# Four edits to a gated recurrence followed by a two-layer network: touched words ahead of the loads, half turns of f, forget ahead of drive, and a last store in two

## The chip, the cores and the metric

The kernel runs on one core of one Trainium2 chip. The metric is the device time of that core in microseconds (us), and lower is better. Before the change the median of nine runs is 398.76 us (397.35 to 399.07).

A core has a matrix engine (TensorE, PE in the profile; PEld is its weight load), a vector engine (VectorE, DVE), an activation engine (ScalarE, ACT), a general engine (GpSimd, POOL), and a sequencer that mostly issues transfers (SyncE, SP). Each runs its own instructions in order and waits on semaphores for the others. Transfers (DMAs) are issued by SP, ACT or POOL and carried out by 16 DMA engines. Matrix results land in PSUM, all other tiles are in SBUF, and inputs and outputs are in HBM.

## What is computed

```python
sig = 1.0 / (1.0 + np.exp(-f_logit))
f = lower_bound[None, None, :] + (1.0 - lower_bound[None, None, :]) * sig
i = 1.0 - f
for t in range(S):
    h = f[:, t] * h + i[:, t] * x[:, t]
    y[:, t] = h
...
h1 = y @ w1
h2 = y @ w2
out = np.maximum(h1, h2) @ w_out
```

x and f_logit are 4 x 6144 x 256 in float32, lower_bound has 256 values, w1 and w2 are 256 x 1024 and w_out is 1024 x 256. The output has 24576 rows of 256. The recurrence runs along the 6144 tokens of each of the four sequences. With y as its result, the second part is a network of two layers whose hidden layer takes the larger of two products.

## The kernel before

The kernel writes the maximum as `h1 + relu(h2 - h1)`. So `wd`, the scaled difference of w2 and w1, feeds a relu, and the linear part `w1 @ w_out` is one 256 x 256 matrix, `w13`. The factor `1 - lower_bound` is taken out of the scan and put into these weights (`om`; `nom` is its negative). Per channel there is then a gate `u = sigmoid(-f_logit)`, a drive `v = u * x`, a forget factor `ff = 1 + nom * u`, and a scan `y = ff * y + v`.

The 24576 tokens are 48 blocks of 512 (`TB`). A block has its channels on the partitions in two halves of 128 (`KC`). Its work on TensorE is eight hidden units, each of two 512-column matmuls (line 254, into a PSUM tile `dT`, of which there are five), and a projection of forty 256-column matmuls (line 277, into `psO`). ACT does the relu of each unit (line 249) and the gate (206). DVE does the drive (210), forget (141), scan (152) and the copies of outputs out of PSUM (326).

**Start.** The loads are issued by SP in the order of the string `LOADS` (line 454). f0a and x0a are the first halves of block 0; w12 is quarter 2 of w1; w22 and w20 are quarters of w2; wo2 is a quarter of w_out. Only `lbr`, the row of lower bounds, is issued by ACT ahead of its first activation (line 570). A handwritten string, `PLAN` (line 458), orders all instructions of blocks 0 to 2 and of the weights, on all engines. In it, `G` is a gate, `V` a drive, `TU` and `TV` turns of u and v on TensorE, `F` a forget, `S` a scan, `RW`, `RO`, `D`, `SC`, `TW` and `KW` prepare weights, `H` is a hidden unit, `R` a relu, and `warm` stands for matmuls on a zero tile that keep TensorE busy. The first instruction of TensorE after the opening warm-up is `keeps_T`, which needs lbr.

**Completion semaphores.** The program uses eight of them in turn for the DMAs of SP and ACT together, in the order in which the program issues them. A DMA that takes a semaphore is issued only when the DMA that had it last has landed.

**Blocks from 3 on.** They reach SBUF by another way, in chunks: three chunks of one block (blocks 3, 4, 5), then chunks of two. `cast` (170) has POOL issue two DMAs that read f and x of a chunk and write them as bf16 to one of two spare places in HBM. `turn_dma` (180) has SP issue two transposing DMAs that bring f and then x of the chunk into SBUF with the channels on the partitions (`fT`, `xT`). `cast_behind` (189) has POOL copy one element of the turned f to `held`, which makes POOL wait for the turn, and then issue the next cast. The first cast waits in the same manner for the second half of x of block 1 (`CA` in the plan).

**Steady loop.** For each block from 3 on and each of its eight units, the loop from line 584 issues the hidden unit, an eighth of the projection of the block before, and at fixed units the copies, the sends (`send_out`, on SP), and for a later block the gate, drive, forget and scan. `gate_of` and `turn_of` say at which unit. SP's order is thus f turn, x turn, then some four sends per chunk. The last block's second half is stored a row set at a time (`store_row`, 339); the sends before it, the last block's first half among them, are `send_out`.

Of the kernel before, what the change touches and what calls it, by code (L numbers as in the profile page):

```python
# [8 lines left out]
FP32 = mybir.dt.float32  # L9
# [3 lines left out]
P = 128  # L13
# [3 lines left out]
def kernel(  # L17
# [13 lines left out]
    nc = tc.nc  # L31
# [4 lines left out]
    KC = D // P  # L36
    FC = DFF // P
    TB = 512
    HB = TB // 2
    NQ = TB // P  # L40
    NBB = S // TB
    NBLK = B * NBB
# [3 lines left out]
    CHUNKS = [(NP + i, 1) for i in range(CB * 2 - 1)]  # L46
# [3 lines left out]
    NS = 2  # L50

    const = ctx.enter_context(tc.tile_pool(name="const", bufs=1))
# [21 lines left out]
    om = const.tile([P, KC], FP32)  # L74
    nom = const.tile([P, KC], FP32)
    lbr = const.tile([KC, P], FP32)
    w1n = wpool.tile([P, KC, DFF], FP32)
    w1b = wpool.tile([P, KC, DFF], BF16)
    w2n = wpool.tile([P, KC, DFF], FP32)
# [10 lines left out]
    def alloc_in(j):  # L90
        fn = inpool.tile([P, NQ, D], FP32, name="fn")
        xn = inpool.tile([P, NQ, D], FP32, name="xn")
        ins[j] = (fn, xn)
        us[j] = natpool.tile([P, NQ, D], BF16, name="un")
        vs[j] = natpool.tile([P, NQ, D], BF16, name="vn")
        ffs[j] = nffpool.tile([P, KC, TB], BF16, name="nff")
        ys[j] = ypool.tile([P, KC, TB], BF16, name="y")

    def load(j, s, half=None):

        src = (f_logit, x)[s]
        q0, q1 = (0, NQ) if half is None else (2 * half, 2 * half + 2)
        nc.sync.dma_start(  # L103
            out=ins[j][s][:, q0:q1, :],
            in_=src[0, j * TB + q0 * P : j * TB + q1 * P, :].rearrange(
                "(q p) d -> p q d", p=P
            ),
        )
# [26 lines left out]
    def forget(o, i, h, on_act=False):  # L135
        if on_act:
            nc.scalar.activation(
                out=o, in_=i, func=AF.Identity, bias=1.0, scale=nom[:, h : h + 1]
            )
            return  # L140
        nc.vector.tensor_scalar(  # L141
            out=o, in0=i, scalar1=nom[:, h : h + 1], scalar2=1.0, op0=ALU.mult, op1=ALU.add
        )

    def scan(j, h, t0, t1, v):
# [18 lines left out]
    spare = {  # L164
        (k, name): scratch.tile([CB * TB, D], BF16, name=f"{name}{k}")
        for k in range(NS)
        for name in ("fs", "xs")
    }

    def cast(c):  # L170
        b0, n = CHUNKS[c]
        b, k = divmod(b0, NBB)
        for name, src in (("fs", f_logit), ("xs", x)):
            nc.gpsimd.dma_start(  # L174
                out=spare[c % NS, name][0 : n * TB, :],
                in_=src[b, k * TB : (k + n) * TB, :],
                max_dma_last_dim=4096,
            )

    def turn_dma(c):  # L180
        n = CHUNKS[c][1]
        for s, name in enumerate(("fs", "xs")):
            t = ttpool.tile([P, KC, CB * TB], BF16, name=("fT", "xT")[s])
            turned[c, s] = t
            nc.sync.dma_start_transpose(  # L185
                out=t[:, :, 0 : n * TB], in_=spare[c % NS, name][0 : n * TB, :]
            )

    def cast_behind(c):

        if c + 1 < NCH:
            last = CHUNKS[c][1] * TB - 1
            nc.gpsimd.tensor_copy(out=held[:], in_=turned[c, 0][:, KC - 1, last : last + 1])  # L193
            cast(c + 1)

# [2 lines left out]
    def part(j, s):  # L198
        c, o = home[j]
        return turned[c, s][:, :, o * TB : (o + 1) * TB]  # L200

    def gate(j):
        ffs[j] = midpool.tile([P, KC, TB], BF16, name="ff")
        ys[j] = ypool.tile([P, KC, TB], BF16, name="y")
        us[j] = midpool.tile([P, KC, TB], BF16, name="u")
        nc.scalar.activation(out=us[j][:], in_=part(j, 0), func=AF.Sigmoid, scale=-1.0)  # L206

    def drive(j):
        vs[j] = midpool.tile([P, KC, TB], BF16, name="v")
        nc.vector.tensor_tensor(out=vs[j][:], in0=us[j][:], in1=part(j, 1), op=ALU.mult)  # L210

    def forget_half(j, h, on_act=False):
        forget(ffs[j][:, h, :], us[j][:, h, :], h, on_act)

    def scan_half(j, h):
        scan(j, h, 0, TB, vs[j][:, h, :])
# [45 lines left out]
    def hidden(j, fc):  # L262
        hidden_whole(j, fc)
        relu(j, fc)
# [49 lines left out]
    def project(j, slot):  # L314
        i, half_ = divmod(slot, 2)
        n = FC + KC
        project_steps(j, i, half_ * n // 2, (half_ + 1) * n // 2)

    osbs = {}

    def copy_out(j, g, on_act=False):
# [3 lines left out]
        else:  # L325
            nc.vector.tensor_copy(out=osbs[j, g][:], in_=pos[j, g, 0][:])  # L326

    def send_out(j, g):
        r0 = j * TB + 2 * g * P
        nc.sync.dma_start(  # L330
            out=out[r0 : r0 + 2 * P, :].rearrange("(p r) d -> p r d", r=2),
            in_=osbs[j, g][:],
        )

    def store(j, g):
        copy_out(j, g)
        outs.append((j, g))

    def store_row(j, g, r):
        osb = lastpool.tile([P, D], FP32, name="row")  # L340
        nc.vector.tensor_copy(out=osb[:], in_=pos[j, g, r][:, 0, :])  # L341
        r0 = j * TB + 2 * g * P
        nc.sync.dma_start(
            out=out[r0 : r0 + 2 * P, :].rearrange("(p r) d -> p r d", r=2)[:, r, :],
            in_=osb[:],
        )
# [4 lines left out]
    def weight_load(k, w, src):  # L351
        cols = slice(k * QF, (k + 1) * QF)
        nc.sync.dma_start(
            out=w[:, :, cols], in_=src[:, cols].rearrange("(h p) f -> p h f", p=P)
        )

    def wout_load(k):
        nc.sync.dma_start(
            out=won[:, 2 * k : 2 * k + 2, :],
            in_=moe_w_out[k * QF : (k + 1) * QF, :].rearrange("(q p) c -> p q c", p=P),  # L360
        )
# [78 lines left out]
    def keep_warm(n):  # L440
        for _ in range(n):
            nc.tensor.matmul(  # L442
                idle[:].rearrange("p r d -> p (r d)"),
                lhsT=warm[:, 0:P],
                rhs=warm[:],
                start=True,
                stop=True,
            )
# [5 lines left out]
    LOADS = """  # L454
# [22 lines left out]
    def load_item(name):  # L477
        if name[:2] == "wo":
            wout_load(int(name[2]))
        elif name[0] == "w":  # L480
            w, src = ((w1n, moe_w1), (w2n, moe_w2))[int(name[1]) - 1]
            weight_load(int(name[2]), w, src)
        else:
            half = ("ab".index(name[2]),) if len(name) == 3 else ()
            load(int(name[1]), "fx".index(name[0]), *half)
# [3 lines left out]
    def send_pending(n):  # L489

        for _ in range(min(n, len(outs))):
            send_out(*outs.pop(0))
# [74 lines left out]
    with tc.manual_schedule():  # L567
        for j in range(NP):
            alloc_in(j)
        nc.scalar.dma_start(out=lbr[:], in_=lower_bound.rearrange("(h p) -> h p", p=P))  # L570
        for name in LOADS.split():
            load_item(name)
        nc.vector.memset(warm[:], 0.0)  # L573
        make_identity(nc, ident[:])
        nc.vector.tensor_copy(out=ident_b[:], in_=ident[:])
        keep_warm(7)
        for item in PLAN.split():
            issue(item)
        for c in range(1, 4):
            cast_behind(c)  # L580
            if c < 3:
                turn_dma(c + 1)

        for j in range(3, NBLK + 1):
            for fc in range(FC):
                if j < NBLK:
                    hidden(j, fc)
                project(j - 1, fc)
                if fc == 0 and j > 3:
                    store(j - 2, 1)  # L590
                if fc == 4 and j < NBLK:
                    store(j - 1, 0)
                if j > 4 and fc in (0, 4):
                    send_pending(2)
                if j == NBLK and fc in (3, 5, 7):
                    if fc == 3:
                        store(j - 1, 0)
                        send_pending(2)
                    else:
                        store_row(j - 1, 1, (fc - 5) // 2)  # L600
                if (j, fc) in gate_of:
                    b = gate_of[j, fc]
                    gate(b)
                    drive(b)
                    for h in range(KC):
                        forget_half(b, h)
                        scan_half(b, h)
                if (j, fc) in turn_of:
                    turn_dma(turn_of[j, fc])
                    cast_behind(turn_of[j, fc])  # L610
# [30 lines left out]
```

## Time and profile before

| | |
|---|---|
| median of nine runs | 398.76 us |
| lowest and highest | 397.35 and 399.07 us |
| time of the profiled execution | 398.48 us |
| span of it, first to last instruction | 396.7 us |
| TensorE clock granted | 1.0 of full |
| bytes moved by DMA | 79.12 MB |
| share of 16 DMA engines: queue of SP / of POOL | 58.2% / 36.4% |
| busy share of DMA engines, 0 to 25, 25 to 57, 57 to 103 us | 0.93, 0.86, 1.12 |

The busy time of an engine is the time in which an instruction of it runs. A wait is the idle time ahead of an instruction, put down to what came last. The chain of waits follows the program back from its last instruction, and at each step goes to what released it. Profile lines in the timeline and the chain begin with the start in us and the length in us; in the timeline a run of like instructions is merged (x4), and the brackets at the end hold the idle time ahead of the first and its releaser. The list of waits gives the sum in us, the number of waits and the longest. The share of DMA can pass 1, since packets of several queues overlap on an engine.

### The profile page before, as it was taken

The numbers are of one execution on the slowest core, as the hardware profiler recorded it, in microseconds if no ns is written. First come the engines' busy times: TensorE is split into PE (matmuls) and PEld (weight loads), VectorE is DVE, ScalarE is ACT, GpSimd is POOL, SyncE is SP. The second block draws the span as 40 slices with busy tenths as digits, with TensorE's granted clock in tenths as the row PEclk, the third lists the DMA queues.
The fourth block names the chain that finished last, engine by engine and source line by source line (L and its number), as shares of the span: only waits on it lengthen the run. The fifth ranks groups of instructions, "written<-read, shape, count | busy, mean of one in ns | idle before, by whom it ended". The sixth has DMA issues, their size and how long they took to land.

```text
span 396.7 us, 7107 instructions
## 1 busy us (share of the span) xinstructions
PE 387.3 (98%) x2779; PEld 273.5 (69%) x2825; DVE 251.3 (63%) x363; ACT 272.8 (69%) x450; POOL 38.4 (10%) x87
## 2 busy tenths in 40 slices
PE   7999999999999999999999999999999999999996
PEld 3786766676677766677776767777676777767675
DVE  4986756737865675577557656765675577567622
ACT  4877666765867766766676677667766766676661
POOL 1611110110111011011011011011011010100000
PEclk9999999999999999999999999999999999999999
DMA  8968899999999999999999999999999899991122
GB/s 240 348 155 145 158 225 236 249 222 235 217 212 251 188 237 172 272 209 219 195 201 239 198 200 203 219 220 206 202 203 201 207 190 196 226 187 54 55 81 107
DMA packets 126486, 79.12 MB, mean 199 GB/s; under 512 B 96370, under 2 KB 102772, under 8 KB 126452
## 3 DMA queue, kind: packets, MB, share of 16 engines
q1 hardware_dynamic: 114160, 55.06, 58.2%
q0 software_dynamic: 12288, 23.60, 36.4%
q8 instruction: 22, 0.36, 0.4%
q14 instruction: 12, 0.10, 0.1%
q10 hardware_dynamic: 4, 0.00, 0.0%
HBM read 53.48 MB, written 48.76 MB: 258 GB/s over the span
## 4 chain that ended last, share of the span: by engine, by line
PE 73%; DMA 23%; issue 1%; ACT 1%; POOL 0%; SPq 0%; DVE 0%; POOLq 0%; ACTq 0%
PE psO L277 42%; PE dT L254 32%; DMA fs<-in_f_logit_dram 10%; DMA fT<-fs 9%; DMA xn<-in_x_dram 2%; DMA w2n<-in_moe_w_dram 2%; DMA w1n<-in_moe_w_dram 1%; ACT rt L249 0%; POOL held L193 0%; ACT u L206 0%; SPq L103 0%; DVE row L341 0%; SPq L185 0%; POOL held L544 0%; POOLq L193 0%
## 5 line engine op out<-in xcount | busy, mean ns | idle before, releaser
L249 ACT ACTIVATE rt<-dT 128x512 bf16<-128x512 f32 x381 | 221.8, 597 | 102.2 <-PE dT L254 100.6
L277 PE MATMUL psO<-wob,rt 128*128 128x256 bf16 x1536 | 230.0, 273 | 0.7 <-ACT rt L249 0.2
L277 PEld LDWEIGHTS <-rt 128*128 128x128 bf16 x1536 | 150.2, 98 | 96.7 <-issue 1.6
L254 PE MATMUL dT<-y,wd 128*128 128x512 bf16 x690 | 208.6, 379 | 2.8 <-DVE y L152 0.5
L152 DVE TENSOR_TENSOR_SCAN y<-ff,y,v 128x512 bf16<-128x512 bf16 x84 | 107.7, 1283 | 2.9
L326 DVE COPY osb<-psO 128x512 f32<-128x512 f32 x93 | 62.7, 679 | 60.3 <-PE psO L277 60.3
L254 PEld LDWEIGHTS <-wd 128*128 128x128 bf16 x736 | 72.0, 98 | 9.4
L210 DVE TENSOR_TENSOR v<-u,xT 128x1024 bf16<-128x1024 bf16 x45 | 31.1, 692 | 71.0 <-ACT u L206 49.8
L277 PE MATMUL psO<-w,y 128*128 128x256 bf16 x384 | 72.6, 273 | 0.0
L206 ACT ACTIVATE u<-fT 128x1024 bf16<-128x1024 bf16 x45 | 47.2, 1050 | 5.8 <-DMA fT<-fs 5.8
L277 PEld LDWEIGHTS <-y 128*128 128x128 bf16 x384 | 37.5, 98 | 4.3
L193 POOL CAST held<-fT 128x1 f32<-128x1 bf16 x23 | 4.7, 206 | 283.6 <-DMA fT<-fs 283.6
L141 DVE TENSOR_SCALAR ff<-u,nom 128x512 bf16<-128x512 bf16 x90 | 30.5, 340 | 0.0
L174 POOL DMA_DIRECT2D fs<-in_f_logit_dram x24 | 13.3, 555 | 5.6 <-issue 5.5
L174 POOL DMA_DIRECT2D xs<-in_x_dram x24 | 13.1, 547 | 0.0
L234 PE MATMUL dT<-y,wd 128*128 128x256 bf16 x64 | 9.9, 273 | 0.0
L442 PE MATMUL psO<-warm 128*128 128x512 bf16 x24 | 7.7, 452 | 1.2 <-DVE warm L573 1.2
L152 DVE TENSOR_TENSOR_SCAN y<-ff,v 128x512 bf16<-128x512 bf16 x6 | 7.3, 1225 | 0.2
L152 DVE TENSOR_TENSOR_SCAN y<-nff,y,dT 128x256 bf16<-128x256 bf16 x10 | 6.9, 733 | 0.2
L116 DVE TENSOR_TENSOR vn<-un,xn 128x512 bf16<-128x512 bf16 x6 | 4.1, 686 | 4.2 <-DMA xn<-in_x_dram 4.2
L234 PEld LDWEIGHTS <-wd 128*128 128x128 bf16 x64 | 6.0, 98 | 1.0 <-ACT wd L399 0.4
L442 PEld LDWEIGHTS <-warm 128*128 128x128 bf16 x24 | 2.4, 110 | 3.6 <-issue 1.4
(41 smaller groups left out, 50.1 us busy)
## 6 DMA issues: line engine op xcount, KB each, us to landing
out_dram<-osb SPq DMA_DIRECT2D x95, 256.0 KB, 3.4
fs<-in_f_logit_dram POOLq DMA_DIRECT2D x21, 512.0 KB, 7.0
xs<-in_x_dram POOLq DMA_DIRECT2D x21, 512.0 KB, 10.2
fn<-in_f_logit_dram SPq DMA_DIRECT2D x4, 256.0 KB, 5.7
xn<-in_x_dram SPq DMA_DIRECT2D x4, 256.0 KB, 5.6
w1n<-in_moe_w_dram SPq DMA_DIRECT2D x4, 256.0 KB, 6.0
w2n<-in_moe_w_dram SPq DMA_DIRECT2D x4, 256.0 KB, 6.0
won<-in_moe_w_out_dram SPq DMA_DIRECT2D x4, 256.0 KB, 6.3
```

The costliest lines, as they stand in the source:

```text
L141: nc.vector.tensor_scalar(out=o, in0=i, scalar1=nom[:, h : h + 1], scalar2=1.0, op0=ALU.mult, op1=ALU.add)
L152: nc.vector.tensor_tensor_scan(out=ys[j][:, h, t0:t1], data0=ffs[j][:, h, t0:t1], data1=v, initial=initial, op0=ALU.mult, op1=ALU.add,)
L174: nc.gpsimd.dma_start(out=spare[c % NS, name][0 : n * TB, :], in_=src[b, k * TB : (k + n) * TB, :], max_dma_last_dim=4096,)
L193: nc.gpsimd.tensor_copy(out=held[:], in_=turned[c, 0][:, KC - 1, last : last + 1])
L206: nc.scalar.activation(out=us[j][:], in_=part(j, 0), func=AF.Sigmoid, scale=-1.0)
L210: nc.vector.tensor_tensor(out=vs[j][:], in0=us[j][:], in1=part(j, 1), op=ALU.mult)
L234: nc.tensor.matmul(dts[j, fc][:, tok], lhsT=wd[:, kc, unit(fc)], rhs=ys[j][:, kc, tok], start=(first and kc == 0), stop=(not first and kc ...
L249: nc.scalar.activation(out=rt[:], in_=dts[j, fc][:], func=AF.Relu)
L254: nc.tensor.matmul(dts[j, fc][:], lhsT=wd[:, kc, unit(fc)], rhs=ys[j][:, kc, :], start=(kc == 0), stop=(kc == KC - 1),)
L277: nc.tensor.matmul(ps, lhsT=lhsT, rhs=rhs, start=start, stop=stop, skip_group_check=True)
L326: nc.vector.tensor_copy(out=osbs[j, g][:], in_=pos[j, g, 0][:])
L442: nc.tensor.matmul(idle[:].rearrange("p r d -> p (r d)"), lhsT=warm[:, 0:P], rhs=warm[:], start=True, stop=True,)
```

## The change

1. **Touches.** Four small DMAs are issued by ACT ahead of all loads. Each reads one float of 16 rows: of x every 32nd of the first 512 rows, of w1 and w2 every 16th of 256, of w_out every 64th of 1024. Nothing reads what they bring. The load of `lbr` moves from ACT to SP, to third place behind f0a and x0a.
2. **Half turns.** For chunks of one block the f turn becomes two DMAs of 256 rows, and `held` reads the last token of the first one. The x turn and chunks of two blocks stay as they were.
3. **Forget, then drive.** In the steady loop both forgets of a block are issued ahead of its drive; the scans follow.
4. **Last block.** The send of the last block's first half becomes two DMAs, one for each row set.

```diff
@@ turn_dma
-            nc.sync.dma_start_transpose(
-                out=t[:, :, 0 : n * TB], in_=spare[c % NS, name][0 : n * TB, :]
-            )
+            cut = HB if n == 1 and s == 0 else n * TB
+            for t0 in range(0, n * TB, cut):
+                nc.sync.dma_start_transpose(
+                    out=t[:, :, t0 : t0 + cut], in_=spare[c % NS, name][t0 : t0 + cut, :]
+                )
@@ cast_behind
-            last = CHUNKS[c][1] * TB - 1
+            n = CHUNKS[c][1]
+            last = (HB if n == 1 else n * TB) - 1
@@ send_out
+    def rows_out(j, g):
+        r0 = j * TB + 2 * g * P
+        return out[r0 : r0 + 2 * P, :].rearrange("(p r) d -> p r d", r=2)
+
     def send_out(j, g):
...
+        if j == NBLK - 1:
+            for r in range(2):
+                nc.sync.dma_start(out=rows_out(j, g)[:, r, :], in_=osbs[j, g][:, r, :])
+        else:
+            nc.sync.dma_start(out=rows_out(j, g), in_=osbs[j, g][:])
@@ start
+    touch = const.tile([16, 4], FP32)
...
-        nc.scalar.dma_start(out=lbr[:], in_=lower_bound.rearrange("(h p) -> h p", p=P))
-        for name in LOADS.split():
+        for k, src in enumerate((x[0], moe_w1, moe_w2, moe_w_out)):
+            rows = TB if k == 0 else src.shape[0]
+            nc.scalar.dma_start(out=touch[:, k : k + 1], in_=src[0 : rows : rows // 16, 0:1])
+        for k, name in enumerate(LOADS.split()):
             load_item(name)
+            if k == 1:
+                nc.sync.dma_start(out=lbr[:], in_=lower_bound.rearrange("(h p) -> h p", p=P))
@@ steady loop
                     gate(b)
+                    for h in range(KC):
+                        forget_half(b, h)
                     drive(b)
                     for h in range(KC):
-                        forget_half(b, h)
                         scan_half(b, h)
```

More of the change, by code (lines that the diff above doesn't have):

```diff
@@ L326, in copy_out @@
             nc.vector.tensor_copy(out=osbs[j, g][:], in_=pos[j, g, 0][:])
+    def rows_out(j, g):
+        r0 = j * TB + 2 * g * P
+        return out[r0 : r0 + 2 * P, :].rearrange("(p r) d -> p r d", r=2)
     def send_out(j, g):
[L329 to L333, printed above, removed]
+        if j == NBLK - 1:
[3 more added lines that the diff above has]
+            nc.sync.dma_start(out=rows_out(j, g), in_=osbs[j, g][:])
     def store(j, g):
```

## The prediction

> **What bounds the kernel now.** I read the page's busy shares first, then the list of waits, then the chain of waits by stretch, and last the timeline where TensorE stands still.
>
> ```profile
> PE 387.3 (98%) x2779; PEld 273.5 (69%) x2825; DVE 251.3 (63%) x363; ACT 272.8 (69%) x450; POOL 38.4 (10%) x87
> ```
>
> TensorE is the bound: 387.3 of 396.7 us. No edit takes a matmul away, so all there is to win lies in its pauses (and pauses that modelled ends hide), and in the start. In the timeline one unit of two 512-column and five 256-column matmuls repeats every 0.98 us from 103 us on, without a pause. The pauses are earlier. At the start:
>
> ```profile
> 7.55 0.40 PE L405 MATMUL dT<-ident_b,w1b 128*128 128x128 bf16 x4 [0.72 <-ACT w1b L364]
> 12.40 0.60 PE L422 MATMUL psO<-wob,w1T 128*128 128x256 bf16 x4 [0.56 <-DVE wob L364]
> 21.51 0.60 PE L422 MATMUL psO<-wob,w1T 128*128 128x256 bf16 x4 [0.19 <-DVE wob L364]
> ```
>
> All three end when a weight that came by DMA has been rounded, so the start follows the landings. The DMA view of 0 to 10 us, in slices of 0.25 us, shows that these are not at full speed:
>
> ```profile
> GB/s 0 0 0 0 0 0 4 78 127 131 360 356 381 377 324 172 160 213 205 246 262 258 340 320 361 352 332 221 250 229 295 332 377 381 361 365 369 369 369 361
> ```
>
> After 370 GB/s at 2.5 to 3.5 us, the rate falls to 160 to 260 until 5.5 us, when the first quarter of w1 is read, and again to 220 to 300 at 6.75 to 7.75 us, when the first of w2 is. Later quarters of both run at 360. Against 360 GB/s the first dip (7 slices, 172 to 258) lost about 0.26 MB or 0.7 us, the second (4 slices) about 0.11 MB or 0.3 us.
>
> The other pauses are at 58 to 102 us. Waits of ACT and DVE in 40 to 110 us, then the chain and the first pause:
>
> ```profile
> ACT u L206 <- DMA fT<-fs: 5.8, 3, 2.4
> ```
>
> ```profile
> DVE v L210 <- DMA xT<-xs: 7.4, 2, 3.9
> ```
>
> ```profile
> 24.93 3.49 DMA fT<-fs
> ...
> 29.00 3.57 DMA fs<-in_f_logit_dram
> 32.58 3.00 DMA fT<-fs
> ...
> 36.15 3.66 DMA fs<-in_f_logit_dram
> 39.83 3.42 DMA fT<-fs
> ...
> 43.82 4.91 DMA fs<-in_f_logit_dram
> ...
> 48.87 4.60 DMA fT<-fs
> ```
>
> ```profile
> 58.70 0.38 PE L254 MATMUL dT<-y,wd 128*128 128x512 bf16 x1
> 59.59 0.38 PE L254 MATMUL dT<-y,wd 128*128 128x512 bf16 x1 [0.51 <-DVE y L152]
> ```
>
> The reader should see a relay: cast f in HBM, turn it into SBUF, let POOL notice (`held`), cast the next. One chunk takes 7.15 to 7.7 us and the engines run behind it: block 6, whose x landed at 55.66, is wanted by TensorE at 58.9 and ready at 59.5. Start to start, against the undisturbed spacing, TensorE loses 0.67 us at 58.7, 0.21 at 75.0, 0.35 at 91.1 and 0.68 at 99.9 to 101.3: **1.9 us**. The last three follow ACT's waits for fT at 69.45, 85.60 and 98.75 (1.0, 2.3, 2.4 us).
>
> **What the Trainium skill says.** "DMA: Bandwidth & Descriptors", section "Queues, rings and completion order": SP and ACT each have a ring on the same 16 DMA engines, and an engine takes packets from its rings in turn. So the touches, issued by ACT, can run beside the loads of SP; that they cost nothing is not said, and before has only the two data packets of lbr on ACT's queue. The same page, "Why a DMA increments its semaphore by 16 and not by 1": the slowest dimension sets how many engines take part; 16 rows give 16 engines, lbr's two rows two (the page's queue 10 has 4 packets, two of data and two of semaphores, which agrees). "ScalarE: Activation LUTs", section "What ACT_TABLE_LOAD costs": 1283 ns; the trace has 1283. No page says why a first read would be slow.
>
> **The change part by part.**
>
> *Touches, cost on ACT.* One ACT issue (0.73 to 1.27) becomes four. SP spaces its own by 0.51 us, so they end near 2.8 us; the table load (1.28) follows until 4.05, and the first gate starts at about 4.1, not 3.60. That is 0.5 us late, and lbr, now third on SP behind x, lands near 4.5 (TensorE wanted it at 4.29). Both are hidden: V0a goes from 4.40 to 4.75, TV0a to about 5.5, the six warm-up matmuls end at 7.0, and the next instruction waits for w1 until 7.55 in any case. If the waits for w1 vanish, up to 0.2 us of it shows.
>
> *Touches, cost on SP.* Eight completion semaphores go round over the loads of both queues, so four more DMAs shift who waits for whom: f0b is now issued only after x's touch has landed, x0b after f0a (3.55), w22 after w1's touch, w10 after x0a (4.35), w20 and wo2 after the other touches. Before, none of the first eight waited. In the packets, f0a starts 1.1 us after its issue. f0a, x0a and w12 keep the engines busy from 1.85 to about 4.1 us at 360 GB/s, so f0b has to be issued by 3.0. x's touch, issued at 0.73, should land near 2.5 to 3 (a first packet at 1.7, a slow one of f0a takes 0.6). x0b at 3.55 is ready at 4.65 and wanted at 4.85. It fits, with 0.2 us to spare.
>
> *Touches, gain.* Bounds: 1.0 us of landings (both dips gone) down to a loss (touches stall the engines just as long, and SP starves: +0.6). I take half a microsecond, because the dips show no cause, the touches have to pay for the same first reads, and the margin on SP is thin. Landings set the three starting pauses and the first cast (it waits for x1b at 18.9), so a shift passes through. **-0.5 us (-1.0 to +0.6).**
>
> *Half turns.* SP issues a 512-row turn in 1.34 us and it lands after 3.49. Packets start 1.1 us in and move about 190 KB in a us, so half of f lands about 0.7 to 1.1 us sooner: half the issue or half of 256 KB. The next cast (0.45 us of POOL, then about 1 us to the first packet) starts as xT ends, where the DMA view of 26 to 46 us (slices of 0.5 us) shows holes now: 7 GB/s at 29.0 and 29.5, 41 and 70 at 37.0 and 37.5, 0 to 45 at 44.0 to 45.0. So there is room. Three single blocks give 3 x 0.9 = 2.7 us at chunk 3 (2.0 to 3.3). Each costs one more issue of about 0.3 us of fixed part on SP, ahead of xT; SP then only waits for casts. After chunk 3 the chunks are gated whole, as before, and keep the lead as long as outputs on SP don't hold the turns: before 92.90 SP's last send was at 91.60, so there the lead is capped near 2.
>
> *Forget, then drive.* Same DVE work: 0.69 + 2 x 0.34 + 2 x 1.28. Where x is late, 0.68 us moves ahead of its landing (block 6: 59.5 to 58.9, the first pause). Where u is late, the second scan ends when it did; the first ends 0.34 later, and TensorE needs both within 0.2 us. Nothing.
>
> *The 1.9 us.* The first pause goes twice over. The others need 1.0, 2.3 and 2.4 us of lead at ACT, and by then TensorE arrives up to 1.2 us earlier itself; with 2 to 2.7 us of lead a wait of some 1 us is left at 98, and five PSUM buffers for hidden units take most of that. **-1.5 us (-1.9 to -0.6).**
>
> *Last send in two.* SP issues two DMAs of about 0.4 us at 392.1; they are through by 393.0, when the first row's send at 392.97 wants SP. The last one, at 394.05, sets the end. 0 (-0.1 to +0.1).
>
> Sum: 398.48 (span 396.70 and 1.78 around it) - 2.0 = 396.5. The median of the runs, 398.76, is 0.28 above the profiled one; I set 396.6.
>
> **Rivals.**
> - *All of it works*: 398.5 - 1.0 - 1.9 = 395.6. For it: the dips are only at first reads. Against: what is said above on thin margins.
> - *Touches give nothing, the relay does*: 398.5 - 1.5 = 397.0. The dips may belong to rows at 4 KB pitch read cold, not to the first word.
> - *No change, 398.5*: the earlier cast only takes DMA time from the second half and xT (the page has DMA at 9 in nearly every slice after 50 us), and the touches cancel. Against: the three holes.
> - *Slower*: SP stands at f0b, x0b and w22 behind touches. Each us past 3.0 is a us on all landings. To be slower than before by 0.8 us it must outweigh 1.5 of gain: x's touch would have to land 2.3 us late, at 5.3, 4.6 us after its issue; at 6.0 the time is 398.5 + 3.0 - 1.5 = 400.0. For it: slow packets are in the trace in this very stretch, and loads then took 5 us or more. Against: those waited behind 0.5 MB of others in their ring.
>
> **How the numbers follow.** Forecast 0.45, all works 0.17, relay alone 0.15, no change 0.13, slower 0.10. Below 398.0 (0.2% is 0.8 us, about what a measurement tells) lie the first two and most of the third: 0.75. The range 395.1 to 398.9 takes in the bounds of the first four and leaves about 0.15 out, mostly above.
>
> **What would show it.** Right: no dip at 4 to 5.5 us, w1's first rounding before 6.5 (now 6.88), the first cast before 18.7 (now 19.05); casts of chunks 1, 2, 3 at about 27.6, 33.8 and 40.6; no TensorE pause at 58.7, ACT waits for fT below 2 us in sum, and the steady unit reached some 2 us sooner. Wrong: SP idle between 2.3 and 5 us, the first f turn landing as late as before, or fT waits that stay, since then the casts lose to contention what the gate gives.

## The result, and the profile after

The changed kernel takes 401.74 us (median of 17 runs), the kernel before on the same chips 399.27 us (54 runs). The ratio is 1.0062 with a 95% interval of 1.0042 to 1.0083: **slower by 0.6%**, where 0.5% faster was forecast. The profiled execution has a span of 398.8 us against 396.7.

The page of the changed kernel, first lines:

```profile
span 398.8 us, 7097 instructions
## 1 busy us (share of the span) xinstructions
PE 387.5 (97%) x2779; PEld 273.3 (69%) x2825; DVE 246.6 (62%) x363; ACT 272.6 (68%) x450; POOL 39.2 (10%) x87
```

TensorE does the same work in the same 387 us. So the 2.1 us are pauses. The list of waits of the changed kernel (sum in us, number, longest):

```profile
ACT u L210 <- DMA fT<-fs: 8.1, 4, 4.2
DVE v L214 <- DMA xT<-xs: 6.2, 5, 3.4
...
PE psO L281 <- ACT rt L253: 1.9, 3, 1.5
...
PE dT L258 <- DVE y L153: 1.4, 2, 0.8
```

Before, the waits of TensorE in these last two rows were 0.2 and 0.5 us, and ACT's longest wait for f was 2.4 us. The timeline of the changed kernel has the places:

```profile
36.14 0.60 PE L258 MATMUL dT<-y,wd 128*128 128x512 bf16 x2 [0.82 <-DVE y L153]
...
52.72 0.38 PE L258 MATMUL dT<-y,wd 128*128 128x512 bf16 x1 [0.56 <-DVE y L153]
...
100.93 1.06 ACT L210 ACTIVATE u<-fT 128x1024 bf16<-128x1024 bf16 x1 [4.19 <-DMA fT<-fs]
...
102.53 0.28 PE L281 MATMUL psO<-wob,rt 128*128 128x256 bf16 x1 [1.53 <-ACT rt L253]
```

Counted start to start against the undisturbed spacing, TensorE loses 0.98 us at 35.2, 0.72 at 51.9, and 1.70 + 2 x 0.38 at 100.7 to 103. That is 4.2 us after the start, against 1.9 before: 2.3 of loss. The start itself is 0.1 us ahead (a pair of projections at 25.14, before 25.23), and from the last row's copy to the end it is 3.01 us (before 3.09). The sum, +2.1, is the difference of the spans.

Now the relay. The chain of waits of the changed kernel, 17 to 62 us:

```profile
18.57 4.93 DMA fs<-in_f_logit_dram
...
23.51 2.67 DMA fT<-fs
...
26.75 5.47 DMA fs<-in_f_logit_dram
...
32.24 3.50 DMA fT<-fs
...
36.38 4.33 DMA fs<-in_f_logit_dram
...
40.73 2.58 DMA fT<-fs
...
43.94 5.97 DMA fs<-in_f_logit_dram
...
50.06 4.84 DMA fT<-fs
...
55.53 7.47 DMA fs<-in_f_logit_dram
```

The reader should compare this with the chain before, whose casts started at 29.00, 36.15, 43.82 and 54.03. The first gate did what it was meant to: the second cast leaves 2.25 us sooner, at 26.75. But that cast takes 5.47 us where it took 3.57, and of the lead 0.34 us is left at 32.24 (before 32.58). The third cast is already 0.2 us behind, and the one at 55.53 is 1.5 us behind. Chunk 3 comes late, and so does everything after it. The DMA view of the first 60 us has the four kinds of transfer side by side, with the median from issue to landing in the last column. The changed kernel:

```profile
fs<-in_f_logit_dram POOLq DMA_DIRECT2D x3, 256.0 KB, 4.9
xs<-in_x_dram POOLq DMA_DIRECT2D x3, 256.0 KB, 5.5
fT<-fs SPq DMA_TRANSPOSE x7, 2.7
xT<-xs SPq DMA_TRANSPOSE x4, 5.2
```

The kernel before:

```profile
fs<-in_f_logit_dram POOLq DMA_DIRECT2D x3, 256.0 KB, 3.7
xs<-in_x_dram POOLq DMA_DIRECT2D x3, 256.0 KB, 4.6
fT<-fs SPq DMA_TRANSPOSE x4, 3.5
xT<-xs SPq DMA_TRANSPOSE x4, 3.8
```

In the median each half of f lands sooner than a whole f did. All three others got slower by 0.9 to 1.4 us. The x of block 3 shows in the drive that waits for it, here in the kernel before and then in the changed one:

```profile
31.08 0.69 DVE L210 TENSOR_TENSOR v<-u,xT 128x1024 bf16<-128x1024 bf16 x1 [1.89 <-DMA xT<-xs]
```

```profile
32.49 0.69 DVE L214 TENSOR_TENSOR v<-u,xT 128x1024 bf16<-128x1024 bf16 x1 [3.39 <-DMA xT<-xs]
```

### The profile page after: what moved, and what is told of

It is laid out like the page before. It is cut to its first block, busy times and chain, and to the rows that moved or that the text cites. A ratio compares the mean times of both kernels' runs of the same rounds, so it can differ in the third digit from the quotient of the medians.

```text
span 398.8 us, 7097 instructions
## 1 busy us (share of the span) xinstructions
PE 387.5 (97%) x2779; PEld 273.3 (69%) x2825; DVE 246.6 (62%) x363; ACT 272.6 (68%) x450; POOL 39.2 (10%) x87
## 4 chain that ended last, share of the span: by engine, by line
PE 73%; DMA 23%; issue 1%; ACT 1%; ACTq 0%; SPq 0%; POOL 0%; DVE 0%; POOLq 0%
PE psO L281 41%; PE dT L258 31%; DMA fs<-in_f_logit_dram 11%; DMA fT<-fs 8%; DMA w2n<-in_moe_w_dram 2%; DMA xn<-in_x_dram 1%; DMA touch<-in_moe_w_out_dram 1%; ACT rt L253 0%; ACTq L581 0%; ACT u L210 0%; POOL held L197 0%; SPq L361 0%; DVE row L349 0%; SPq L366 0%; SPq L188 0%
## 5 line engine op out<-in xcount | busy, mean ns | idle before, releaser
L153 DVE TENSOR_TENSOR_SCAN y<-ff,y,v 128x512 bf16<-128x512 bf16 x84 | 103.3, 1272 | 1.5
L142 DVE TENSOR_SCALAR ff<-u,nom 128x512 bf16<-128x512 bf16 x90 | 27.7, 350 | 68.4 <-ACT u L210 68.4
L397 POOL TENSOR_TENSOR wdf<-w2n,w1n 128x256 f32<-128x256 f32 x5 | 4.0, 817 | 8.8 <-DMA w2n<-in_moe_w_dram 8.8
```

Source lines behind the costliest of these rows:

```text
L142: nc.vector.tensor_scalar(out=o, in0=i, scalar1=nom[:, h : h + 1], scalar2=1.0, op0=ALU.mult, op1=ALU.add)
L153: nc.vector.tensor_tensor_scan(out=ys[j][:, h, t0:t1], data0=ffs[j][:, h, t0:t1], data1=v, initial=initial, op0=ALU.mult, op1=ALU.add,)
```

## The experiments

Theory A says that the half turns with their gate are the loss; theory B blames the touches and what they shift in the start. Twelve kernels were run. The first set takes the parts one at a time.

**The half turns and their gate alone.** Edit to the kernel before:

```diff
+            cut = HB if n == 1 and s == 0 else n * TB
+            for t0 in range(0, n * TB, cut):
+                nc.sync.dma_start_transpose(out=t[:, :, t0 : t0 + cut], in_=...[t0 : t0 + cut, :])
...
+            last = (HB if n == 1 else n * TB) - 1
```

> The kernel before with the half turns and the gate on the first half alone. Theory A (a cast issued while the turns of the chunk before are still in flight, and half turns that each cost as much of SP as a whole one, stretch the relay): slower than before by 1.5 to 3.5 us; x of block 3 lands near 32 us and not 29; ACT waits for fT over 7 us in sum. Theory B (the touches and what they move in the start and on the semaphores did it): the same as before or faster by up to 1.5 us, with the casts of chunks 1 to 3 some 1 us earlier each.

Measured: 403.6 us, ratio 1.0103 (1.0068 to 1.0139). Theory A holds, but the loss, about 4.1 us by the ratio, is above its range, and x of block 3 came even later than expected. In the view of the turns of this kernel, 18 to 58 us:

```profile
DMA to landing us min/median/max: 2.5/3.4/8.5
```

The longest of them, 8.5 us, is the x turn of block 3: issued at 27.33, landed at 35.8. The next cast had been issued at 27.81, and its f landed at 35.66. The drive of that block started at 35.91; the profile puts its wait down to an ACT copy that ended at the same moment, but the drive does not use that copy, and x is what it needed last. TensorE waited for the y of that block:

```profile
39.55 0.61 PE L257 MATMUL dT<-y,wd 128*128 128x512 bf16 x2 [3.88 <-DVE y L152]
```

Part of the loss is in no list of waits. The next view gives, for each stretch of 4 us of this kernel, the busy time and number of instructions of PE, PEld, DVE, ACT and POOL, then the granted clock of TensorE, the DMA share and GB/s:

```profile
36.00:40.00 4.00, 0.45 (x3) 0.22 (x4) 4.00 (x7) 0.00 (x0) 0.48 (x2) 1.00 0.45 95
40.00:44.00 4.00, 4.00 (x19) 2.35 (x18) 1.99 (x5) 2.46 (x4) 0.78 (x2) 0.57 1.01 177
44.00:48.00 4.00, 4.00 (x32) 2.82 (x30) 3.63 (x5) 2.28 (x5) 1.02 (x3) 1.00 0.34 76
```

Just behind the wait, TensorE issues 19 matmuls in 4 us instead of 32, at a clock of 0.57. In stretches of 0.5 us the clock is 0.50 from 40.5 to 43.5 us, and 1.00 before 40 and after 44. That costs some 1.7 us (an estimate: 4 us times the missing 0.43) on top of the wait. Four more of the profiles below have one such dip, each in or just behind long waits of TensorE: late gate at 64.9 us, quarters at 48.8, x first at 66.4, and x between the halves at 35.7. The kernel with no cast held back has three. The profiles of the kernel before, of the changed kernel (longest wait 1.5 us) and of the other experiments have none. So a late turn can cost its wait and a dip behind it. That the wait brings the dip is read from their order in time, and no run shows how long a wait it takes: in the quarters, waits of 1.4 and 1.2 us close together brought one at 48.8 us and none at 70.

**The touches alone**, with lbr moved to SP, as in the change.

> The kernel before with the touches and the moved load of lbr alone. Theory A: within 0.8 us of before, since TensorE reaches 25.6 us at the same place in both traces. Theory B: slower by 1.5 us or more. A third reading (the touches are worth what they were meant for): faster by 0.5 to 1 us, with the first cast near 18.5 us.

Measured: 398.62 us, ratio 0.9987 (0.9970 to 1.0004). Theory B falls. The third reading, faster by at least 0.5 us, is neither shown nor excluded. In the trace the first cast left at 18.38 (before 19.05) and TensorE was 0.3 us ahead at 25 us, but single profiles scatter as much: in the two kernels with half turns and no touches, above and below, TensorE was 0.2 and 0.3 us ahead at the same place.

**Forget ahead of drive alone.**

> The kernel before with both forgets ahead of the drive alone. Theory A: within 0.8 us of before, at most 0.6 faster (the pause of TensorE at 58.7 us goes from 0.67 us to about nothing). Theory C (the first scan 0.34 us later delays TensorE in every block): slower by more than 0.8 us, with new pauses on y.

Measured: 398.41 us, ratio 0.9986 (0.9963 to 1.0009). The pause of 0.67 us at 58.7 is down to 0.11: the timeline of this kernel shows the two matmuls of that unit all but back to back.

```profile
58.35 0.70 PE L254 MATMUL dT<-y,wd 128*128 128x512 bf16 x2
```

No pauses on y appeared, so theory C falls.

**Half turns, gate on the second half.** The first edit above without its last line: the next cast waits for the whole f, as before.

> The kernel before with the f turn of single blocks in two halves, the next cast gated on the last token of the second half, as before. It splits theory A. If the cost of the halves themselves (two issues of 1.3 us each, half the rate) is the larger part: slower by 1 us or more, each single-block turn of f landing about 1.3 us later, and the run with the early gate no slower than this one. If the collision of cast and turn is the larger part: within 1 us of before, and the early gate slower than this by 1 us or more.

Measured: 405.47 us, ratio 1.0137 (1.0097 to 1.0177). This answers with the first reading: turning in halves costs more than 1 us with no early cast at all, and the early gate did not make it worse (the intervals of the two overlap). The +1.4% contains the dip of the clock: two of the six executions kept the full clock (a mean of 0.999 or 1.0) and took 401.9 and 402.0 us, the other four took 405.3 to 405.8. Against the executions of the kernel before at full clock (median 398.8 us) the halves cost about 0.8%. SP's timeline of this kernel:

```profile
24.49 2.59 SPq L187 DMA_TRANSPOSE fT<-fs  x2
27.18 2.27 SPq L187 DMA_TRANSPOSE xT<-xs  x1
```

Two issues take 2.59 us where one took 1.34, so x is issued 2.7 us after f and not 1.4. The casts left at 30.63, 39.41 and 49.63.

This kernel and the one with the half turns and their gate differ in the gate alone, so x of block 3 also shows what meeting a cast does to a turn. Time from issue to landing, here and then with the early gate:

```profile
xT<-xs SPq DMA_TRANSPOSE x1, 3.6
```

```profile
xT<-xs SPq DMA_TRANSPOSE x1, 8.5
```

The cast of f that follows took 4.2 us from its issue here (30.63 to 34.85) and 7.9 there (27.81 to 35.66).

The second set asks what a turn costs by itself, and what an early cast does without halves.

**The three other parts together, whole turns and the old gate.**

> The changed kernel with whole turns and the old gate again: touches, forget ahead of drive and the last send in two are kept. If the half turns with their gate are the whole loss: faster than before by 0.5 to 1.5 us (the two parts alone gave ratios of 0.9987 and 0.9986), no pause of TensorE at 58 us above 0.7 us. If the parts harm each other, or the last send in two costs something: no faster than before.

Measured: 398.51 us, ratio 0.9983 (0.9962 to 1.0004). Leaving the half turns and their gate out turns +0.6% into -0.2%, at the edge of what can be told from none. It is within the interval of what the two parts gave alone, so there is no sign that they harm each other.

**Four quarters in place of two halves**, gate on the last (`cut = TB // 4`).

> The kernel before with f of single blocks turned in four quarters, gate on the last. If a turn costs SP about 1.2 us of issue whatever its size: four issues of about 1.2 us, x issued 4.9 us after f's first (1.4 in before, 2.6 with halves), chunk 3 cast about 53 us (43.8 before, 49.6 with halves), time 404 to 412. If the issue goes by size and only the collision costs: four issues of 0.3 to 0.6 us, time within 2 us of before.

Measured: 408.94 us in a single run, as the first reading said: x was issued 5.6 us after f's first piece and chunk 3 cast at 53.91. The view of SP's turns in 18 to 58 us (number, then shortest, median and longest issue in ns, first and last start) of this kernel:

```profile
L187 SPq DMA_TRANSPOSE fT<-fs x12: 1168/1240/2269, 24.1 to 50.8; - x12
```

Of the late-gate kernel, with f turns of 256 rows and one of 1024:

```profile
L187 SPq DMA_TRANSPOSE fT<-fs x7: 1188/1255/1301, 24.5 to 54.9; - x7
```

And of the kernel before, with whole f turns of 512 rows and one of 1024:

```profile
L185 SPq DMA_TRANSPOSE fT<-fs x4: 1225/1399/2263, 24.9 to 48.9; - x4
```

The shortest issue is 1.17 us for 128 rows, 1.19 for 256 and 1.23 for 512. **In these kernels the issue of a turn of 128 to 512 rows costs SP about 1.2 us whatever its size.**

**x first, gate on x**, with whole turns.

```diff
-        for s, name in enumerate(("fs", "xs")):
+        for s, name in ((1, "xs"), (0, "fs")) if n == 1 else ((0, "fs"), (1, "xs")):
...
-            nc.gpsimd.tensor_copy(out=held[:], in_=turned[c, 0][:, KC - 1, last : last + 1])
+            s = 1 if CHUNKS[c][1] == 1 else 0
+            nc.gpsimd.tensor_copy(out=held[:], in_=turned[c, s][:, KC - 1, last : last + 1])
```

> The kernel before with whole turns, for single blocks x first and then f, the next cast gated on x: so the cast goes out while the turn of f is still in flight, as with the half gate, but with no half turns. If collision alone stretches the relay: the turn of f lands 2 us or more later than its issue would say (over 5 us from issue), and f's next cast takes over 5 us. If not: relay of about 6.7 us a chunk instead of 7.4, chunk 3 cast before 43 us.

Measured: 404.91 us in a single run. It missed its question. x landed only at about 30.1 us, so the next cast left at 30.64, later than before and not earlier; later casts followed at 39.49 and 49.66. The experiment does not separate the readings.

**Early casts with whole turns.** The copy that holds the next cast is left out behind the three single-block chunks; the spare places alone pace these.

```diff
+            if CHUNKS[c][1] > 1:
-            nc.gpsimd.tensor_copy(out=held[:], in_=turned[c, 0][:, KC - 1, last : last + 1])
+                nc.gpsimd.tensor_copy(out=held[:], in_=turned[c, 0][:, KC - 1, last : last + 1])
```

> The kernel before, whole turns, without the copy that holds the next cast back behind single-block chunks: those casts go out as soon as their spare place is free. If a cast beside turns stretches both (collision): slower than before by 1 us or more, casts of f taking over 5 us instead of 3.6, turns of single blocks landing after 5 us or more, DMA engines busy for a microsecond with hardly a byte moved. If only the halves are at fault and early casts are good: faster than before by 1 us, chunk 3 in SBUF 3 us sooner than 55.7.

Measured: 396.97 us, ratio **0.9946 (0.9925 to 0.9968)**. The forecast of theory A's collision was wrong here, and the second reading right: casts left at 19.76, 29.58 and 32.79 (before 29.00, 36.15 and 43.82), and f of chunk 3 landed at about 48.5 us (before 53.5). All pauses of TensorE after 58 us are gone. From 24 us to 392 us its list of waits holds one row:

```profile
PE dT L255 <- DVE y L152: 0.7, 1, 0.7
```

That one wait, at 35.2 us, is for block 3, whose x landed at 31.5. There is still stretching (casts and turns took up to 9.4 us from issue to landing), but by then they had been started 7 to 11 us sooner.

The third set looks for the best version and for what the collision is.

**All gains together**: touches, forget ahead of drive, and the free casts.

> The kernel before with the touches, forget ahead of drive, and the casts behind single-block chunks not held back (whole turns). If the gains of the parts stand beside each other: ratio 0.9946 x 0.9987 x 0.9986, so about 0.992 (0.990 to 0.994). If they take from the same pauses: about 0.9946.

Measured: 397.0 us, ratio 0.995 (0.9933 to 0.9968). The second reading fits: TensorE waits for nothing in 24 to 392 us, so forget ahead of drive had no pause left to take. The touches act in the start and show no gain there in this run: its first cast left at 18.90, that of the kernel with free casts alone at 18.55.

**The same, but the first chunk's cast stays held.**

> As the one before it, but the cast behind the first chunk stays held until that chunk's f is turned; only those behind the second and third single-block chunk are free. If the early second cast is what pushes x of block 3 to 31.5 us and so makes the pause of 0.82 us at 34 us: no pause there, and faster by up to 0.8 us than with all three free. If the lead that this cast gives is worth more later on: slower than with all three free, with ACT waiting for fT at 85 to 100 us again.

Measured: 397.56 us, ratio 0.9949 (0.9932 to 0.9967). The same within the interval. Its question fell away, since the run before it has no pause at 35 us to remove: TensorE waits for nothing in 24 to 392 us in either. Holding the first cast brings ACT's waits for f back (3.6 us in sum), and they cost TensorE nothing.

**No cast held back at all**, through the whole kernel.

> As the first of this set, but no cast is held back at all, those of two-block chunks neither: only the two spare places pace them. If a cast beside turns is harmless as long as it is early: no slower than with the single-block ones free. If casts and turns in flight together stretch each other in the steady part too: slower by 1 us or more, with waits for fT after 60 us.

Measured: 433.39 us, ratio 1.0812 (1.0760 to 1.0864). Here the collision shows in the open. The turns of this kernel in 110 to 250 us:

```profile
DMA to landing us min/median/max: 5.7/12.4/17.3
```

The turns of the kernel before in the same stretch:

```profile
DMA to landing us min/median/max: 4.1/5.0/8.2
```

The DMA engines were as busy (share 1.18 against 1.09) and moved less (187 GB/s against 215). Casts and turns in flight together stretch each other in the steady part. The three dips of the clock are part of the 8% too.

**x turned between the two halves of f**, gate on the first half.

> The kernel before with half turns of f in single blocks and the gate on the first half, as in the half-turn run, but SP issues the x turn between the two halves. If the loss of the half turns is x being issued 1.25 us later and falling into the next cast: x of block 3 lands near 29 us, no pause of some 4 us at 35 us, and the time is at least 1.5 us below that of the half-turn run (403.6). If the loss is the half turns' own rate and the early gate: as slow as that run, with waits of ACT for the second half of f in place of DVE's for x.

Measured: 402.59 us, ratio 1.0070 (1.0041 to 1.0100), which is not clearly below the half-turn run. The trace speaks for the second reading:

```profile
34.13 1.06 ACT L208 ACTIVATE u<-fT 128x1024 bf16<-128x1024 bf16 x1 [6.04 <-DMA fT<-fs]
...
35.72 0.53 PE L256 MATMUL dT<-y,wd 128*128 128x512 bf16 x1 [4.17 <-ACT rt L251]
```

Now the second half of f is the turn in flight when the next cast leaves at 27.66. It was issued at 27.13 and landed at 34.1, after 7.0 us. In the half-turn run it was x, after 8.5, and in the changed kernel x, after 6.2. **In all three the turn issued last before the cast is the one that pays.** After that single wait of over 4 us, and the dip of the clock to 0.5 behind it until 39.2 us, TensorE waits for nothing up to 392 us: the relay did get ahead.

## Why the prediction was wrong

*The bound and the pauses.* Right: TensorE bound, pauses of 1.9 us, a relay behind them. Freeing that relay with whole turns gained 0.5% or 2 us, about what the relay was said to be worth.

*Half turns: the first half's landing.* Right in size: 2.67 us after issue for the first chunk against 3.49, a gain of 0.8 where 0.7 to 1.1 was put (both ways of halving that are named there give 0.7; the 1.1 is not worked out).

*Half turns: "Each costs one more issue of about 0.3 us of fixed part on SP".* **This term failed.** I took most of the issue of 1.34 us to go with the rows. Its fixed part is about 1.2 us, and three sizes (128, 256, 512 rows) show it. The halves are therefore issued at half the rate of one whole turn, f as a whole lands later, and x is issued 1.3 us later. With the late gate this alone gave +1.4%, or about 0.8% where the clock stayed full.

*Half turns: "So there is room".* **This step failed too.** I read the holes in the DMA traffic at 29 us as free time for the next cast. Before, the x turn of block 3 was still open in that hole: DVE started its drive at 31.08, on x's landing. In the changed kernel the second cast and this turn met; the cast took 5.47 us in place of 3.57, and the drive started at 32.49. The rival "no change" named this contention, and I set it aside because of the holes. Of the 2.25 us by which the second cast left sooner, 0.34 remained when its f was in place, and the next two rounds lost that and more. The runs with late and early gate do not tell how much of the loss belongs to the halves and how much to the meeting, since their intervals overlap; that both mechanisms are at work is shown, by the late gate and the quarters for the first, and for the second by x of block 3 with late and early gate, by x between the halves and by the unheld casts.

*Touches.* Forecast -0.5 us, measured 0.9987, or -0.5 us with an interval that reaches zero, so the agreement in size may be chance. The delay on ACT was worked out well (first gate at 3.96 us where 4.1 was put). The places look right in part: w1's first rounding began at 6.46 (6.88), the first cast at 18.57 (19.05). But these scatter from profile to profile: in the eight kernels without touches the first cast left at 18.49 to 19.18 us, in the six with them at 18.38 to 18.98, so they show no gain. And the dip itself stayed. The DMA view of the changed kernel, 0 to 10 us in slices of 0.25 us:

```profile
GB/s 0 0 0 0 0 0 0 62 86 221 303 373 345 385 334 138 238 258 221 233 287 152 205 254 250 205 209 279 291 303 324 234 209 242 266 279 340 352 381 389
```

From 3.75 to 8 us it is no better than before (in this kernel the loads moved 2.16 MB in 10 us, before 2.41). The touches also came late for w1: issued at 1.22 and 1.67 us, those of w1 and w2 took 2.7 us in the median, so they landed at about 4 us, while the dip began at 3.75. So an early first read of w1 was hardly tried, and why these reads are slow stays open. The rival with SP held behind touches did not happen: f0b was issued at 2.60 and x0b at 3.52, about as worked out. That rival was my way to "slower", and the slow side came from elsewhere.

*Forget, then drive.* The prediction put the first pause to nothing; alone it left 0.11 us of it, ratio 0.9986 with an interval that reaches 1. *Last send in two*: nothing, as forecast (3.01 us against 3.09 at the end).

*The 1.9 us.* Forecast -1.5, measured +2.3. The term is wrong in sign because the two steps above are.

## What to carry to other kernels

Before a transfer is cut to let its first part go ahead, look for what its issue costs by itself: compare the shortest issues of several sizes in the trace, and do not scale one size. A hole in the traffic is not free time while a transfer still has to land; look at who waits for a landing across the hole. And where a hold-back is suspected, try moving or dropping it for the few places where it costs before refining it: dropping it for three chunks gave 0.5%, dropping it everywhere cost 8%.

## What the hardware showed unasked

A transposing DMA took SP 1.17 to 1.23 us at the least for 128 to 512 rows of 256 bf16 values. A cast from HBM to HBM and a turn in flight together slowed both: the last turn issued before the second cast took 6.2 to 8.5 us to land in three kernels, while the turns of the kernel before in that stretch took 3.0 to 4.6, and with no hold the turns' median went from 5.0 to 12.4 us with busy DMA engines and fewer bytes moved in the same time. In five kernels the granted clock of TensorE fell from 1.0 to 0.5 for some 3.4 us in or just behind waits of TensorE of 1.2 to 4.2 us. While the first quarter of w1 was read the loads ran at 160 to 260 GB/s, later at 360; touches of sixteen words that landed as that read began did not change it.
